# Chunk 0 of a fused attention and expert kernel: up-projection 3 by seven products, banks of its own for each unit, and two turns by transposing transfers

## The chip, the cores and the metric

The kernel runs on one core of a Trainium2 chip. The metric is the device time of one execution in microseconds (us); the profile's span is a little shorter than that time. The engines are named as in the profile: PE (TensorE, the matmul engine), PEld (its weight load), DVE (VectorE), ACT (ScalarE), POOL (GpSimd) and SP (SyncE, which here only issues transfers). PSUM is the memory that PE writes its results to; it has eight banks, and one bank holds 128 x 512 numbers of 4 bytes. SBUF is the large on-chip memory.

## The reference

Attention over pooled keys and values, and then four experts whose outputs are added with weights:

```python
# q, k, v: 8 batches, 8 heads, 576 tokens, 64 dims
k_p = k.reshape(B, H, 72, 8, D).mean(axis=3)      # 72 pooled keys
v_p = v.reshape(B, H, 72, 8, D).mean(axis=3)
attn = softmax(scale * q @ k_p.T)                 # written out in the original
x = (attn @ v_p).transpose(0, 2, 1, 3).reshape(4608, 512)
p = domain_probs / (domain_probs.sum(-1, keepdims=True) + 1e-09)
for e in range(4):
    h = np.maximum(x @ w1[e], 0.0)                # 512 -> 1024
    out += p[:, e:e + 1] * (h @ w2[e])            # 1024 -> 512
```

## The kernel before

**Chunks.** The 4608 tokens are worked in nine chunks of 512. Chunk b, for b from 0 to 7, is the first 512 tokens of batch b; the ninth collects the remaining 64 tokens of each batch. While PE works on the experts of one chunk, the attention of the next batch is woven in between. Everything is bf16 with sums in fp32. For each chunk and expert there is an up-projection (x @ w1[e], the relu, kept in a buffer H) and a down-projection (H @ w2[e], added into acc with the expert's probability).

**Seven products.** Most projections are done by a Strassen-like scheme: a 2 x 2 block product by seven block products instead of eight, at the price of sums of blocks. For an up-projection these are `first_weight_sums(e)` (sums of blocks of w1[e], on DVE), `x_sum(c, n)` (four sums of blocks of x, on DVE) and `up_product(c, e, unit, step)` for step 0 to 6 and unit 0 and 1, each of 4 matmuls of 256 columns (line 681). A unit works in two PSUM banks. What ends a step is: step 0, ACT copies bank 0 into bank 1 (line 694); steps 2 and 3, ACT copies bank 0 to SBUF (`partial`, line 696; in chunk 0 the copies lie in `partial_first`, which is the room of w2[3]); steps 1 and 5, ACT takes the relu (lines 698 and 702); steps 4 and 6, DVE adds a copy and takes the relu (`relu_sum`, line 661). A down-projection is `down(c, e, step)`, seven steps of 8 matmuls (line 749), with `weight_sums(e)` and `hidden_sums(c, e, part)` on DVE. The plain forms are `up` (one fc is 4 matmuls of 512 columns into one bank, line 603) and `down_plain(c, e, r)` (8 matmuls of 512 columns into `chains[r % 2]`, line 775, then an `add` on DVE, line 825).

**Order.** The order of the instructions on each engine is the order in which the program writes them; nothing is moved by a scheduler. Each engine works its list from top to bottom. Waits come from the use of tiles: a matmul that writes a bank waits until the last reader of that bank is done, a reader until the data are there.

**PSUM.** The eight banks are `att` (two), `att_first` (two, in the beginning), `units[1]` (two) and `chains` (two, named o_ps). `units[0]` is allocated only behind chunk 0, in the room that `att_first` leaves. So in chunk 0, `up_product` with unit 0 uses the two banks of `att_first`.

**Chunk 0.** `attention_first()` makes batch 0's attention and the first up-projection, and `first_chunk()` the rest, an order written out by hand: the up-projections 1 (plain), 2 (seven products on both units, the local helper `both(step)`) and 3 (plain, on `units[1]`), the down-projections 0 (seven products), 1 and 2 (plain), and in between the attention of batch 1: `fold_keys(1)`, `queries(1, pair)` (four transposes of a pair of heads on PE and a copy, line 356 and 360), `keys(1)` (line 299), `scores(1, pair)` (line 374, exps on ACT), `context(1, r)` for the four parts r of 128 tokens (line 448, then two DVE instructions of `divide` write `x_tok`, lines 409 and 410), and `turn(1, r)`: four transposes of x_tok on PE (line 466), and a copy by ACT (line 468) into `xT`, the input of chunk 1's up-projections. `two_banks(b)` gives scores and contexts of batches 0 and 1 `att` and `att_first` in turn, and later batches `att`.

From batch 2 on, a turn is a transposing transfer issued by SP, which writes xT straight from x_tok (line 462):

```python
if b >= BUSY:
    nc.sync.dma_start_transpose(out=dst, in_=x_tok)
    return
```

**Loads.** Weights, keys, values and queries are loaded by POOL's queue in the order of the program. `load_w2(3)` follows `both(6)`, since w2[3]'s room is `partial_first` until then; behind it in the queue are `load_wide`, `load_q(2)` and others of batch 2, which wait for `fold_rest`.

**Behind chunk 0** a loop over slots g runs: at slot 0 `up_product(1, 0, 0, 0)` and then `down_plain(0, 2, 3)`; at each later slot two up_products and one `down` step, with pieces of the attention (`later`) and weight sums (`sums`) put at slots of their own. Before the loop, `open_bank` runs one matmul into a bank of the new units[0].

Of the kernel before, what the change touches and what calls it, by code (L numbers as in the profile page):

```python
# [17 lines left out]
def kernel(  # L18
# [231 lines left out]
    def turn_of(what, n):  # L250
        turns[what] += 1
        return turns[what] % n
# [5 lines left out]
        return units[1][turn_of("work", 2)][:]  # L258

    def two_banks(b):  # L260
        return att_first[turn_of("att", 2)] if b < 2 else att

    def one_bank(b):
        return spare_bank() if b == 0 else two_banks(b)[:, 0]
# [25 lines left out]
    def keys(b, hs):  # L290
        state[("kpT", b)] = kpTs[b % 3]
        if b >= BUSY:
            nc.sync.dma_start_transpose(
                out=state[("kpT", b)][:, 0:H], in_=kp_all[:].rearrange("j h a d -> j (h a d)")
            )
            return
        kpt_ps = one_bank(b).bitcast(BF16)[:, 0:H * SP].rearrange("p (h j) -> p h j", j=SP)
        for h in range(hs.start, hs.stop):
            nc.tensor.transpose(kpt_ps[:, h, :], kp_all[0:SP, h], ident[:SP, :SP])
        copy = nc.scalar.copy if b else nc.vector.tensor_copy  # L300
        copy(out=state[("kpT", b)][:, hs, 0:SP], in_=kpt_ps[:, hs])
# [26 lines left out]
        for _ in range(n):  # L328
            nc.tensor.matmul(w_ps[:, 0:cols], lhsT=zeros[:, 0:P], rhs=zeros[:, 0:cols])

    def open_bank(ps):

        nc.tensor.matmul(ps, lhsT=ident[:], rhs=w1_bf[:, 0, 0, 0:NT], skip_group_check=True)

    def values_folds(b):
        raw = raw_v if b >= BUSY else raws[("vraw", b)]
        return (folds(raw) if b < BUSY else []) + [lambda: nc.vector.tensor_add(
# [4 lines left out]
    def queries(b, pair=0):  # L342
        q_sb = raws[("q", b)]
        if pair == 0:
            state[("qT", b)] = apool.tile([P, H, 2, P], BF16, name="qT")
        if b >= BUSY:
            nc.sync.dma_start_transpose(
                out=state[("qT", b)][:].rearrange("p h a t -> p (h a) t"),
                in_=q_sb[:].rearrange("p h r d -> p (h r d)"),
            )  # L350
            return
        bank = one_bank(b) if b else att_first[pair % 2][:, 0] if pair >= 2 else chains[(pair + 1) % 2][:]
        qt_ps = bank.bitcast(BF16)[:, 0:4 * P].rearrange("p (h a t) -> p h a t", h=2, a=2)
        for hh in range(2):
            for rr in range(2):
                nc.tensor.transpose(
                    qt_ps[:, hh, rr, :], q_sb[:, 2 * pair + hh, 2 * rr:2 * rr + 2, :], ident[:]
                )
        copy = nc.scalar.copy if pair in ((1, 3), (1, 2))[b] else nc.vector.tensor_copy
        copy(out=state[("qT", b)][:, 2 * pair:2 * pair + 2], in_=qt_ps)  # L360

    def key_columns(b, h, lo):

# [24 lines left out]
            func=ACT.Exp, scale=EXP_SCALE,  # L388
        )

    def scores_of_two(b, pair):


        scores(b, pair, 0)
        banks = [unit[1][:] for unit in units]
        score_products(b, pair + 1, banks)
        for r2 in range(2):
            nc.scalar.activation(
                out=state[("expT", b)][:, 2 * pair + 2:2 * pair + 4, :, r2].rearrange("j h a t -> j (h a) t"),
                in_=banks[r2][0:SP].rearrange("j (h t) -> j h t", t=P),  # L400
                func=ACT.Exp, scale=EXP_SCALE,
            )
# [53 lines left out]
    def turn(b, r):  # L456
        if ("xT", b) not in state:
            state[("xT", b)] = xpool.tile([P, KC, NT], BF16, name="xT")
        x_tok = state.pop(("x", b, r))[:].rearrange("p a h d -> p (a h d)")
        dst = state[("xT", b)][:, :, r * P:(r + 1) * P]  # L460
        if b >= BUSY:
            nc.sync.dma_start_transpose(out=dst, in_=x_tok)
            return
        xt_ps = (units[1][0][:] if b else att_first[1][:, 0] if r == 3 else chains[0][:]).bitcast(BF16)[:, 0:KC * P].rearrange("p (k t) -> p k t", t=P)
        for kc in range(KC):
            nc.tensor.transpose(xt_ps[:, kc, :], x_tok[:, kc * P:(kc + 1) * P], ident[:])
        copy = nc.vector.tensor_copy if b == 0 and r == 3 else nc.scalar.copy
        copy(out=dst, in_=xt_ps)
# [194 lines left out]
    def up_product(c, e, unit, step):  # L663
        b11, b21, t3, b22 = weight_parts(e)
        a11, _, a12, a22 = x_parts(c)
        t, s, s3 = wu_bf[:, e], state[("xs", c)], third_sum(c)
        banks = units[unit] or [att_first[1][:, i] for i in range(2)]
        bank, grows, lhs, rhs = [
            (0, False, b11, a11),
            (1, True, b21, a12),  # L670
            (0, True, t[:, 1], s[:, 1]),
            (0, True, t3, s3),
            (1, False, t[:, 0], s[:, 0]),
            (0, True, t[:, 2], a22),
            (1, True, b22, s[:, 2]),
        ][step]
        ps = banks[bank][:]
        for n in range(2):
            for kc in range(HK):
                f = (2 * unit + n) * P  # L680
                nc.tensor.matmul(  # L681
                    ps[:, n * HN:(n + 1) * HN], lhsT=lhs[:, kc, f:f + P], rhs=rhs[:, kc, :],
                    start=(not grows and n == 0 and kc == 0), stop=(kc == HK - 1),
                    skip_group_check=True,
                )
        part = (partial if c else partial_first)[:, unit]
        H_sb = hidden[(c, e)]

        def quarter(f, tok):
            return H_sb[:, f, tok, 2 * unit:2 * unit + 2, :].rearrange("p i n -> p (i n)")  # L690

        if step == 0:

            nc.scalar.copy(out=banks[1][:], in_=ps)  # L694
        elif step == 2 or step == 3:
            nc.scalar.copy(out=part[:, step - 2], in_=ps)  # L696
        elif step == 1:
# [154 lines left out]
    def first_chunk():  # L852
# [5 lines left out]

        sums = {e: first_weight_sums(e) for e in range(E)}

        def both(step):
            for unit in range(2):
                up_product(0, 2, unit, step)

        each(*(lambda n=n: x_sum(0, n) for n in range(4)), *sums[0][0:3])
        norm_probs()
# [2 lines left out]
        hidden_sums(0, 0, 1)  # L869
        up(0, 1, (2, 3))  # L870
        each(*sums[1][0:3])
        up(0, 1, (4,), bank=att_first[1][:, 1])
        each(sums[2][0], sums[2][1], sums[2][3], sums[2][2])
        up(0, 1, (5,), bank=chains[0])
        both(0)
        up(0, 1, (6,), bank=chains[1])
        both(1)
        up(0, 1, (7,), bank=chains[0])
        last_sum = weight_sums(0)
        each(sums[0][3], sums[1][3], *last_sum[0:2])  # L880
        both(2)
        down(0, 0, 0)
        both(3)
        hidden_sums(0, 0, 2)
        down(0, 0, 1)
        both(4)
        hidden_sums(0, 0, 3)
        down(0, 0, 2)
        both(5)
        each(*last_sum[2:])  # L890
        down(0, 0, 3)
        both(6)
        load_w2(3)
        up(0, 3, (0,), bank=units[1][0])
        down(0, 0, 4)
        sums[3][0]()
        fold_keys(1)
        up(0, 3, (1, 2, 3))
        down(0, 0, 5)
        sums[3][1]()  # L900
        down(0, 0, 6)
        up(0, 3, (4,))
        queries(1, 0)
        queries(1, 1)
        sums[3][2]()
        up(0, 3, (5,))
        keys(1, every)
        queries(1, 2)
        up(0, 3, (6,))
        queries(1, 3)  # L910
        up(0, 3, (7,))
        scores(1, 0)
        scores(1, 1)
        each(*weight_sums(1)[0:3])
        down_plain(0, 1, 0)
        fold_first, *fold_rest = values_folds(1)
        fold_first()
        scores(1, 2)
        scores(1, 3)
        each(*fold_rest)  # L920
        load_wide(0, 0)
        load_q(2)
# [20 lines left out]
        each(*weight_sums(3)[0:3])  # L943
        down_plain(0, 2, 2)
        turn(1, 3)
        each(*(lambda n=n: x_sum(1, n) for n in range(4)))

    def pieces_later():


        at, amid = {}, {}

        def put_amid(slot, piece):
            amid[slot] = piece
# [59 lines left out]
    with tc.manual_schedule(  # L1014
# [13 lines left out]
        load_w2(0)  # L1028
        load_w1(3)
        attention_first()  # L1030
        load_whole(1, k, "kraw")
        load_q(1)
        load_w2(1)
        load_whole(1, v, "vraw")
        load_w2(2)
        first_chunk()
        psum_first.__exit__(None, None, None)
        psum_last = ctx.enter_context(
            tc.tile_pool(name="psum_last", bufs=1, space=bass.MemoryType.PSUM))
        units[0] = [psum_last.tile([P, NT], F32, name=f"unit0{i}") for i in range(2)]  # L1040
        open_bank(units[0][1][:])

        N = len(order)
        later, amid = pieces_later()
        below_of = [(0, 3)] + order
        sums = {}
        for at, pieces in (((3,), weight_sums(3)[3:]), ((8,), weight_sums(1)[3:]), ((10, 15, 22, 14), weight_sums(2)),
                           ((15,), first_weight_sums(3)[3:])):  # L1050
            for slot, piece in zip(at, pieces, strict=True):
                sums.setdefault(slot, []).append(piece)
        POOLED = (4,)
# [55 lines left out]
```

The softmax here doesn't subtract the row's maximum and nothing guards it: scores larger than these inputs give would overflow.

## Time and profile before

The time before is 491.87 us, the median of 3 runs (491.71 to 492.28). The profiled execution spans 489.4 us.

| | busy us | share of the span |
|---|---|---|
| PE | 481.7 | 98% |
| PEld | 410.3 | 84% |
| DVE | 376.7 | 77% |
| ACT | 304.3 | 62% |
| POOL | 116.4 | 24% |

PE and PEld overlap: the next weights are loaded while a matmul runs. The busy time of matmuls overlaps too, as they are pipelined: the profile gives a matmul of 256 columns 273 ns, though in a dense stretch the next one begins sooner. So the cost of a group of matmuls is read from start to start. A line of the timeline gives the start, the duration, the engine, the source line, the operation, output and inputs, the shape and the count; "idle before" in brackets is what the engine waited for. In the stage that is changed, PE goes through up-projection 3 from 40.5 us, the scores of batch 1 about 51.3 and 53.7, the contexts and turns between 57.7 and 66.6, and chunk 1 from 66.8.

### The profile page before, as it was taken

How to read it: one execution, taken by the hardware profiler on the slowest of the kernel's cores; microseconds unless marked ns; L12 is line 12 of the kernel's file. 1: busy time of each engine (PE TensorE's matmuls, PEld its weight loads, DVE VectorE, ACT ScalarE, POOL GpSimd, SP SyncE). 2: the span in 40 equal slices, each digit the busy share in tenths (PEclk: the TensorE clock that was granted, in tenths of full speed). 3: DMA queues.
4: the chain of work that ended last, by engine and by line, in shares of the span. 5: the costliest groups of instructions: out<-in, count | busy, mean ns of one | idle time of the engine just before them, and what ended most of it. 6: DMA issues, size and time to landing. Idle time of an engine off the chain costs nothing.

```text
span 489.4 us, 11544 instructions
## 1 busy us (share of the span) xinstructions
PE 481.7 (98%) x4694; PEld 410.3 (84%) x4701; DVE 376.7 (77%) x758; ACT 304.3 (62%) x580; POOL 116.4 (24%) x115
## 2 busy tenths in 40 slices
PE   8999999999999999999999999999999999999996
PEld 4867568898888888888889888888888888888885
DVE  5778799799768976798679866897678766876674
ACT  4776546855685567657665567556755566556650
POOL 8320323242423055015321452111011101010100
PEclk9999999999999999999999999999999999999999
DMA  9999998995887579544954298311111010004003
GB/s 196 212 209 205 197 173 127 110 89 62 96 116 60 88 74 139 45 79 54 163 50 90 26 158 74 68 23 65 35 23 23 23 66 2 13 21 87 1 1 87
DMA packets 101828, 41.97 MB, mean 86 GB/s; under 512 B 73856, under 2 KB 100224, under 8 KB 101776
## 3 DMA queue, kind: packets, MB, share of 16 engines
q0 software_dynamic: 56944, 22.42, 41.5%
q1 hardware_dynamic: 43728, 17.77, 16.5%
q10 hardware_dynamic: 1104, 1.05, 0.6%
q8 instruction: 37, 0.61, 0.5%
q14 instruction: 15, 0.12, 0.1%
HBM read 45.69 MB, written 9.44 MB: 113 GB/s over the span
## 4 chain that ended last, share of the span: by engine, by line
PE 96%; POOL 1%; DMA 1%; issue 0%; DVE 0%; POOLq 0%
PE o_ps L749 41%; PE unit L681 41%; PE o_ps L775 3%; PE unit L603 2%; PE att L448 1%; PE unit L808 1%; DMA wt_bf<-in_v_dram 1%; PE att L374 1%; PE o_ps L603 1%; POOL wt_bf L141 1%; PE unit L618 1%; PE att_first L681 1%; PE unit L374 0%; PE o_ps L618 0%; PE att L502 0%
## 5 line engine op out<-in xcount | busy, mean ns | idle before, releaser
L825 DVE SCALAR_TENSOR_TENSOR acc<-o_ps,p_all,acc 128x256 f32<-128x256 f32 (+1 forms) x285 | 127.0, 485 | 52.5 <-PE o_ps L749 37.9
L749 PEld LDWEIGHTS <-H 128*128 128x128 bf16 x1320 | 129.1, 98 | 15.2
L681 PEld LDWEIGHTS <-w_bf 128*128 128x128 bf16 x1056 | 102.2, 98 | 12.7 <-issue 0.2
L661 DVE CUSTOM_DVE_ANT_0 H<-unit,partial 128x512 bf16<-128x512 f32 x128 | 87.2, 684 | 26.1 <-ACT partial L696 12.6
L749 PE MATMUL o_ps<-w_bf,H 128*128 128x256 bf16 x792 | 102.6, 273 | 0.0
L681 PE MATMUL unit<-xT,w_bf 128*128 128x256 bf16 x680 | 97.5, 273 | 0.0
L696 ACT COPY partial<-unit 128x512 f32<-128x512 f32 x128 | 72.3, 592 | 30.0 <-PE unit L681 30.0
L763 POOL TENSOR_TENSOR acc<-acc,addend 128x512 f32<-128x512 f32 x24 | 30.4, 1265 | 253.7 <-ACT addend L761 203.3
L681 PEld LDWEIGHTS <-wu_bf 128*128 128x128 bf16 x792 | 75.3, 98 | 11.4 <-issue 2.5
L681 PE MATMUL unit<-xs,wu_bf 128*128 128x256 bf16 x512 | 77.0, 273 | 0.0
L749 PE MATMUL o_ps<-wt_bf,H 128*128 128x256 bf16 x528 | 68.4, 273 | 0.0
L698 ACT ACTIVATE H<-unit 128x512 bf16<-128x512 f32 x64 | 38.8, 606 | 31.5 <-PE unit L681 31.5
L749 PEld LDWEIGHTS <-S 128*128 128x128 bf16 x528 | 51.7, 98 | 6.2
L702 ACT ACTIVATE H<-unit 128x512 bf16<-128x512 f32 x64 | 38.5, 602 | 25.8 <-PE unit L681 25.6
L694 ACT COPY unit<-unit 128x512 f32<-128x512 f32 x65 | 37.8, 582 | 22.0 <-PE unit L681 17.3
L681 PE MATMUL unit<-xs,w_bf 128*128 128x256 bf16 x256 | 38.4, 273 | 0.0
L823 ACT ACTIVATE acc<-o_ps,p_all 128x256 f32<-128x256 f32 x72 | 30.6, 485 | 10.3 <-PE o_ps L749 8.5
L151 POOL DMA_DIRECT2D kraw<-in_k_dram x20 | 26.4, 1319 | 41.8 <-DMA kraw<-in_k_dram 41.8
L681 PE MATMUL unit<-xT,wu_bf 128*128 128x256 bf16 x228 | 34.2, 272 | 0.0
L749 PE MATMUL o_ps<-w_bf,S 128*128 128x256 bf16 x264 | 34.2, 273 | 0.0
L749 PE MATMUL o_ps<-wt_bf,S 128*128 128x256 bf16 x264 | 34.2, 273 | 0.0
L151 POOL DMA_DIRECT2D vraw<-in_v_dram x20 | 28.9, 1443 | 18.2 <-DMA vraw<-in_v_dram 17.7
(170 smaller groups left out, 517.6 us busy)
## 6 DMA issues: line engine op xcount, KB each, us to landing
out_dram<-acc SPq DMA_DIRECT2D x32, 256.0 KB, 4.6
w_bf<-in_moe_w_dram POOLq DMA_DIRECT2D x6, 1024.0 KB, 20.7
q_sb<-in_q_dram POOLq DMA_DIRECT2D x7, 512.0 KB, 10.0
vraw<-in_v_dram POOLq DMA_DIRECT2D x22, 144.0 KB, 6.6
kraw<-in_k_dram POOLq DMA_DIRECT2D x21, 144.0 KB, 6.3
w_bf<-in_moe_w_dram POOLq DMA_DIRECT2D x4, 512.0 KB, 13.5
wt_bf<-in_k_dram POOLq DMA_DIRECT2D x4, 144.0 KB, 5.7
wt_bf<-in_v_dram POOLq DMA_DIRECT2D x4, 144.0 KB, 4.5
```

Source lines behind the costliest of these rows:

```text
L151: nc.gpsimd.dma_start(out=raw[:], in_=rows_of(src, b, 2 * part, 2 * part + 2), accum_op=ALU.add if part else ALU.bypass)
L603: nc.tensor.matmul(out_ps, lhsT=w1_bf[:, e, kc, fc * P:(fc + 1) * P], rhs=xT[:, kc, at], start=(kc == 0), stop=(kc == KC - 1), skip_group_ ...
L661: nc.vector._custom_dve(TENSOR_ADD_SAT, out=dst, in0=ps, in1=part, s0=LARGEST, s1=0.0)
L681: nc.tensor.matmul(ps[:, n * HN:(n + 1) * HN], lhsT=lhs[:, kc, f:f + P], rhs=rhs[:, kc, :], start=(not grows and n == 0 and kc == 0), stop ...
L694: nc.scalar.copy(out=banks[1][:], in_=ps)
L696: nc.scalar.copy(out=part[:, step - 2], in_=ps)
L698: nc.scalar.activation(out=quarter(0, 0), in_=ps, func=ACT.Relu)
L702: nc.scalar.activation(out=quarter(0, 1), in_=ps, func=ACT.Relu)
L749: nc.tensor.matmul(ps[:, j], lhsT=lhs[:, i, j * P:(j + 1) * P], rhs=rhs[:, i, :], start=(not grows and i == 0 and j == 0), stop=(i == HF - 1),
L763: nc.gpsimd.tensor_add(out=dst, in0=dst, in1=addend[:])
L823: nc.scalar.activation(out=dst, in_=o_ps, func=ACT.Copy, scale=prob)
L825: nc.vector.scalar_tensor_tensor(out=dst, in0=o_ps, scalar=prob, in1=dst, op0=ALU.mult, op1=ALU.add,)
```

## The change

There are four parts.

1. Up-projection 3 of chunk 0 is made by seven products on both units, instead of 32 plain matmuls of 512 columns. `both(e, step)` now takes the expert, and goes through units 1, 0 for expert 3. The four sums of w1[3]'s blocks are all made in chunk 0; the last of them stood at slot 15. `load_w2(3)` follows `both(3, 6)`, which is the last use of `partial_first`.
2. `units[0]` is allocated before chunk 0's second half, and `att_first` is given back there. Both units have banks of their own in chunk 0, and `open_bank` goes. Batch 1's attention then has `att` alone: the queries go four heads at a time through one bank (`queries_of_two`), the keys through `chains[1]`, the scores two pairs at a time through `att` and bank 0 of both units (`scores_of_two`, which later batches have already), and the contexts all through `att`.
3. `turn(1, 0)` and `turn(1, 1)` become transposing transfers; `turn(1, 2)` and `turn(1, 3)` stay on PE.
4. `x_sum(1, 3)` moves from the end of `first_chunk` behind the work of slot 0.

Its purpose is to have fewer and shorter matmuls on PE between the second half of chunk 0 and chunk 1.

```diff
     def two_banks(b):
-        return att_first[turn_of("att", 2)] if b < 2 else att
+        return att if b else att_first[turn_of("att", 2)]
...
-        kpt_ps = one_bank(b).bitcast(BF16)[:, 0:H * SP].rearrange("p (h j) -> p h j", j=SP)
+        kpt_ps = (chains[1][:] if b else spare_bank()).bitcast(BF16)[:, 0:H * SP].rearrange("p (h j) -> p h j", j=SP)
...
-    def open_bank(ps):
-
-        nc.tensor.matmul(ps, lhsT=ident[:], rhs=w1_bf[:, 0, 0, 0:NT], skip_group_check=True)
...
+    def queries_of_two(pair, bank, copy):
...
+        for hh in range(4):
+            for rr in range(2):
+                nc.tensor.transpose(
+                    qt_ps[:, hh, rr, :], q_sb[:, 2 * pair + hh, 2 * rr:2 * rr + 2, :], ident[:]
+                )
+        copy(out=state[("qT", 1)][:, 2 * pair:2 * pair + 4], in_=qt_ps)
...
-    def scores_of_two(b, pair):
-        scores(b, pair, 0)
-        banks = [unit[1][:] for unit in units]
+    def scores_of_two(b, pair, bank=1):
+        scores(b, pair, 0 if b > 1 else None)
+        banks = [unit[bank][:] for unit in units]
...
-        if b >= BUSY:
+        if b >= BUSY or (b == 1 and r < 2):
             nc.sync.dma_start_transpose(out=dst, in_=x_tok)
             return
...
-        banks = units[unit] or [att_first[1][:, i] for i in range(2)]
+        banks = units[unit]
...
-        def both(step):
-            for unit in range(2):
-                up_product(0, 2, unit, step)
+        def both(e, step):
+            for unit in (1, 0) if e == 3 else (0, 1):
+                up_product(0, e, unit, step)
...
-        both(6)
-        load_w2(3)
-        up(0, 3, (0,), bank=units[1][0])
-        down(0, 0, 4)
-        sums[3][0]()
-        fold_keys(1)
-        up(0, 3, (1, 2, 3))
-        down(0, 0, 5)
-        sums[3][1]()
-        down(0, 0, 6)
-        up(0, 3, (4,))
-        queries(1, 0)
-        queries(1, 1)
-        sums[3][2]()
-        up(0, 3, (5,))
-        keys(1, every)
-        queries(1, 2)
-        up(0, 3, (6,))
-        queries(1, 3)
-        up(0, 3, (7,))
-        scores(1, 0)
-        scores(1, 1)
+        both(2, 6)
+        each(*sums[3][0:2])
+        both(3, 0)
+        down(0, 0, 4)
+        both(3, 1)
+        each(sums[3][3], sums[3][2])
+        fold_keys(1)
+        down(0, 0, 5)
+        both(3, 2)
+        down(0, 0, 6)
+        both(3, 3)
+        queries_of_two(0, att[:, 0], nc.scalar.copy)
+        both(3, 4)
+        both(3, 5)
+        keys(1, every)
+        queries_of_two(2, chains[0][:], nc.vector.tensor_copy)
+        both(3, 6)
+        load_w2(3)
+        scores_of_two(1, 0, 0)
         each(*weight_sums(1)[0:3])
         down_plain(0, 1, 0)
         fold_first, *fold_rest = values_folds(1)
         fold_first()
-        scores(1, 2)
-        scores(1, 3)
+        scores_of_two(1, 2, 0)
         each(*fold_rest)
...
-        each(*(lambda n=n: x_sum(1, n) for n in range(4)))
+        each(*(lambda n=n: x_sum(1, n) for n in range(3)))
...
-        at, amid = {}, {}
+        at, amid = {0: [lambda: x_sum(1, 3)]}, {}
...
         attention_first()
+        psum_first.__exit__(None, None, None)
+        psum_last = ctx.enter_context(
+            tc.tile_pool(name="psum_last", bufs=1, space=bass.MemoryType.PSUM))
+        units[0] = [psum_last.tile([P, NT], F32, name=f"unit0{i}") for i in range(2)]
...
         first_chunk()
-        psum_first.__exit__(None, None, None)
-        psum_last = ctx.enter_context(
-            tc.tile_pool(name="psum_last", bufs=1, space=bass.MemoryType.PSUM))
-        units[0] = [psum_last.tile([P, NT], F32, name=f"unit0{i}") for i in range(2)]
-        open_bank(units[0][1][:])
...
-        for at, pieces in (((3,), weight_sums(3)[3:]), ((8,), weight_sums(1)[3:]), ((10, 15, 22, 14), weight_sums(2)),
-                           ((15,), first_weight_sums(3)[3:])):
+        for at, pieces in (((3,), weight_sums(3)[3:]), ((8,), weight_sums(1)[3:]), ((10, 15, 22, 14), weight_sums(2))):
```

More of the change, by code (lines that the diff above doesn't have):

```diff
@@ L351, in queries @@
             return
-        bank = one_bank(b) if b else att_first[pair % 2][:, 0] if pair >= 2 else chains[(pair + 1) % 2][:]
+        bank = att_first[pair % 2][:, 0] if pair >= 2 else chains[(pair + 1) % 2][:]
         qt_ps = bank.bitcast(BF16)[:, 0:4 * P].rearrange("p (h a t) -> p h a t", h=2, a=2)
@@ L358, in queries @@
                 )
-        copy = nc.scalar.copy if pair in ((1, 3), (1, 2))[b] else nc.vector.tensor_copy
+        copy = nc.scalar.copy if pair % 2 else nc.vector.tensor_copy
         copy(out=state[("qT", b)][:, 2 * pair:2 * pair + 2], in_=qt_ps)
+    def queries_of_two(pair, bank, copy):
+        q_sb = raws[("q", 1)]
+        if pair == 0:
+            state[("qT", 1)] = apool.tile([P, H, 2, P], BF16, name="qT")
+        qt_ps = bank.bitcast(BF16)[:, 0:8 * P].rearrange("p (h a t) -> p h a t", h=4, a=2)
+        for hh in range(4):
[4 more added lines that the diff above has]
+        copy(out=state[("qT", 1)][:, 2 * pair:2 * pair + 4], in_=qt_ps)
     def key_columns(b, h, lo):
@@ L871, in first_chunk @@
         each(*sums[1][0:3])
-        up(0, 1, (4,), bank=att_first[1][:, 1])
+        up(0, 1, (4,), bank=units[0][1][:])
         each(sums[2][0], sums[2][1], sums[2][3], sums[2][2])
         up(0, 1, (5,), bank=chains[0])
-        both(0)
+        both(2, 0)
         up(0, 1, (6,), bank=chains[1])
-        both(1)
+        both(2, 1)
         up(0, 1, (7,), bank=chains[0])
@@ L880, in first_chunk @@
         each(sums[0][3], sums[1][3], *last_sum[0:2])
-        both(2)
+        both(2, 2)
         down(0, 0, 0)
-        both(3)
+        both(2, 3)
         hidden_sums(0, 0, 2)
         down(0, 0, 1)
-        both(4)
+        both(2, 4)
         hidden_sums(0, 0, 3)
         down(0, 0, 2)
-        both(5)
+        both(2, 5)
         each(*last_sum[2:])
         down(0, 0, 3)
-        both(6)
-        load_w2(3)
-        up(0, 3, (0,), bank=units[1][0])
-        down(0, 0, 4)
-        sums[3][0]()
-        fold_keys(1)
-        up(0, 3, (1, 2, 3))
-        down(0, 0, 5)
-        sums[3][1]()
-        down(0, 0, 6)
-        up(0, 3, (4,))
-        queries(1, 0)
-        queries(1, 1)
-        sums[3][2]()
-        up(0, 3, (5,))
-        keys(1, every)
-        queries(1, 2)
-        up(0, 3, (6,))
-        queries(1, 3)
-        up(0, 3, (7,))
-        scores(1, 0)
-        scores(1, 1)
+        both(2, 6)
[15 more added lines that the diff above has]
+        both(3, 6)
+        load_w2(3)
+        scores_of_two(1, 0, 0)
         each(*weight_sums(1)[0:3])
```

## The prediction

> **What bounds the kernel now.** I read the page first, for the busy shares and the chain that ended last.
>
> ```profile
> PE 481.7 (98%) x4694; PEld 410.3 (84%) x4701; DVE 376.7 (77%) x758; ACT 304.3 (62%) x580; POOL 116.4 (24%) x115
> ...
> DMA  9999998995887579544954298311111010004003
> ...
> PE 96%; POOL 1%; DMA 1%; issue 0%; DVE 0%; POOLq 0%
> ```
>
> PE is 98% busy and 96% of the chain, so a change is worth the PE time it removes, less the PE waits it brings. The second row says that the DMA engines are full in the first seven slices, some 85 us, and the change puts two transfers there. Next, busy time by stretches:
>
> ```profile
> 40.50:66.80 26.30, 25.98 (x200) 14.66 (x203) 21.87 (x39) 12.76 (x22) 6.46 (x8) 1.00 1.30 199
> ...
> 80.00:470.00 390.00, 390.00 (x3813) 344.15 (x3812) 302.49 (x609) 251.89 (x483) 87.62 (x75) 1.00 0.49 66
> ```
>
> The columns are the stretch, its length, then PE, PEld, DVE, ACT and POOL busy, clock, DMA share, GB/s. The changed stretch is 40.5 to 66.8. From 80 us on PE has no gap at all: whatever the change makes of the moment when chunk 1's first up_product starts (66.79) is carried unchanged to the end. So I compute that moment. PE's timeline has the pieces:
>
> ```profile
> 40.54 1.03 PE L603 MATMUL unit<-xT,w_bf 128*128 128x512 bf16 x3
> ...
> 42.28 2.75 PE L603 MATMUL unit<-xT,w_bf 128*128 128x512 bf16 x12
> 44.87 1.04 PE L749 MATMUL o_ps<-w_bf,H 128*128 128x256 bf16 x8
> 45.74 1.04 PE L749 MATMUL o_ps<-wt_bf,H 128*128 128x256 bf16 x8
> ...
> 66.35 0.39 PE L466 MATMUL unit<-ident,x_tok 128*128 128x128 bf16 x4
> 66.58 0.38 PE L333 MATMUL unit<-w_bf,ident 128*128 128x512 bf16 x1
> 66.79 0.60 PE L681 MATMUL unit<-xT,w_bf 128*128 128x256 bf16 x4
> ```
>
> Durations overlap, so I price by start to start: twelve of 512 columns in 2.59 us are 216 ns each, eight of 256 in 0.87 us are 109 ns each, one turn (four transposes) is 0.23, open_bank 0.21.
>
> Last, what a transposing transfer takes. Below are stretches around some issues of the existing turns, and the landing of the one at 194.65 and of the one at 162.30:
>
> ```profile
> 61.00:64.00 3.00, 2.95 (x25) 1.64 (x24) 2.94 (x6) 0.59 (x1) 1.76 (x3) 1.00 1.35 195
> 64.00:67.00 3.00, 3.00 (x29) 1.81 (x28) 2.91 (x6) 0.81 (x2) 0.00 (x0) 1.00 1.52 193
> ...
> 194.60:197.60 3.00, 3.00 (x30) 2.70 (x28) 2.64 (x6) 1.36 (x4) 1.18 (x1) 1.00 1.43 88
> ```
>
> ```profile
> xT<-x_tok SPq DMA_TRANSPOSE x1, 5.6
> ...
> xT<-x_tok SPq DMA_TRANSPOSE x1, 2.4
> ```
>
> The median of the 24 is 2.5 us. Those issued while loads ran are slower: 101.34 took 6.9, 143.48 6.3, 194.65 5.6, 298.09 6.0, and 156.56 and 246.84 3.8 and 3.9. Where the new ones fall (59 to 68 us) the share is 1.35 to 1.52, as high as the worst of these.
>
> **What the Trainium skill says.** "DMA: Bandwidth & Descriptors", Queues, rings and completion order: each DMA engine takes turns between the queue rows it has work for, packet by packet. The trace agrees: from 195.8 to 196.3 the loads' queue ran 149 packets and the transposes' 109. The same page, Why a DMA increments its semaphore by 16 and not by 1: every engine posts its own last increment after its data, so the slowest of 16 engines sets the landing; the 5.6 to 6.9 us beside loads fit. "TensorE: Matmul & The Clock Gate", Back-to-back issue gap, gives N/2.4 + 2.5 ns, 109 and 216 ns here: the trace has just that (its other figure, 131 ns for 512 columns in a stream, the trace doesn't bear out).
>
> **The change part by part.**
> PE work. Up-projection 3 was 8 x 4 = 32 matmuls of 512 columns: 6.93 us. As seven products on two units it is 56 of 256: 6.11. Two turns less: 0.45. open_bank gone: 0.21. Sum: 0.82 + 0.45 + 0.21 = 1.48 us less. queries_of_two, keys and scores_of_two do the same transposes and products as before in other banks: nothing on PE.
> Units' own banks before 40.5 us: PE was busy 18.45 of 18.50 us from 22 to 40.5, so nothing to gain.
> Waits inside expert 3. up_product step 1 accumulates onto the copy that ACT makes of step 0, and that copy must wait until DVE's relu_sum of expert 2's step 6 has left the bank (41.01 + 0.68 = 41.69). Two copies at 0.58, the second 0.5 later, end at 42.3 and 42.8; PE comes at 42.28 and 42.7: 0.2 us of waiting, with down(0,0,5) queued behind. The later steps alternate with downs or transposes and find ACT and DVE done.
> More on DVE: four relu_sums of 0.6 (ACT did relus before) and one more weight sum, moved from slot 15. The four queries copies become one of 1024 columns on each of ACT and DVE. By my count DVE ends its last relu_sum at 51.8 (PE ends both(3,6) at 50.8), then three sums of weights 1 (2.1 before: 50.99 to 53.13), an add (0.67), folds and vp (2.3: 54.49 to 56.80) and the add of down_plain(0,1,1) (0.67): 57.5. PE has passed context(1,0) at 57.1 and wants that bank for down_plain(0,1,3): 0.45 us waiting, with context(1,1) behind it.
> att alone for the four contexts: x_tok of one must be out before the next. PE puts 1.73 us of down_plain and 0.26 of context between; add, inv, x_tok on DVE take 0.67 + 0.23 + 0.69 = 1.6. It just fits: nothing.
> Arrival at up_product(1,0,0,0): from 40.54 the old work sums to 25.87 (6.93 + three downs 2.62 + 7 plain 12.12 + contexts 1.04 + turns 0.88 + queries 0.88 + scores 0.92 + keys 0.26 + 0.21), that is 0.38 of gaps in 26.25. The new is 24.4 + 0.2 + 0.45 + 0.15 of small gaps: 65.7 instead of 66.8. Without more, 1.1 us won.
> load_w2(3) must now wait for the last use of partial_first, which lies in it: issued at 52 instead of 42.23. But the loads in this queue land in turn: weights 2 of w2 at 57.8, this one at 63.6 before. Issued at 52 it still stands behind weights 2, and DVE reads it at 65: nothing.
> The two transfers. up_product(1,0,0,0) reads tokens 0 to 255, just turns 0 and 1; PE, in order, stands there, with down_plain(0,2,3) and all of chunk 1 behind it. x_tok(1,1) is out at 61.1 (61.50 before; it gains little as DVE is late). It has 4.6 us until PE arrives. Bounds from the trace: 2.4 (quiet) to 6.9 (loads). I take 6.6, near the upper end: loads fill the engines to beyond 69 us, and turn(1,0), issued at 59.0, stands ahead in the same queue. Landing 67.7, PE starts at 67.75: 2.0 us of waiting against 1.1 won. Net +1.0: 492.9.
> Two ACT copies of turns go (1.2 us), two exps come (0.6 each), x_sum(1,3) goes behind the add of slot 0: ACT is 12.76 of 26.3 busy, and both hide behind PE's wait.
>
> **The rivals.**
> Transfers get through, 490.7: they land within 4.6 us, as at 156.56 and 246.84 (3.8, 3.9). For it: in the trace the transposes' packets are small (256 B), and loads were accumulating in the slow cases, plain here. Against: fuller engines, two in one queue. Then only 1.1 to 1.2 us is won.
> Middle, 491.9: the second takes 5 to 6.2, as at 194.65 and 298.09, landing 66.1 to 67.3. The wait just eats the gain.
> load_w2(3) becomes the wait, 495: if its 21.4 us runs from issue, it lands at 73 and down(0,3,0) (69.83 before) waits some 3 us. Against: the landings in turn.
>
> **How the numbers follow.** Forecast case 47% (41 slower, 6 within 0.2%, as +0.2% is 492.85), middle 22% (18 within, 2 each side), transfers get through 26% (25 faster, 1 within), w2 5% (slower). Faster 0.27, same 0.25, slower 0.48. The range, from 490.6 (all fast) to 494.0 (the second transfer at 7.7), leaves out the w2 case and some tails.
>
> **What would show it.** Right: a PE gap ahead of L691 at 66 to 68 us released by the transfer xT<-x_tok, two such issues near 59 and 61 with 5.5 to 7.5 us to landing, a PE wait near 57 released by a DVE add. Wrong: landings below 4.6 and PE going straight on near 65.7; or DVE waiting for w2.

## The result and the profile after

The changed kernel takes 497.60 us (median of 6 executions, 495.79 to 498.87) against 491.98 for the kernel before (6 executions, 491.71 to 492.31) on the same chip. The ratio is 1.0111, 95% interval 1.0089 to 1.0132: slower by some 5.6 us. Forecast was 492.9, with a range from 490.6 to 494.0. The profiled execution of the changed kernel took 498.32 us, with a span of 496.4.

The page of the changed kernel, the lines that answer to those shown of before, with the granted clock of PE over the 40 slices as well:

```profile
PE 483.7 (97%) x4716; PEld 412.8 (83%) x4716; DVE 378.9 (76%) x761; ACT 303.8 (61%) x581; POOL 116.4 (23%) x115
...
PE   8999969999999999999999999999999999999995
...
PEclk9999979999999999999999999999999999999999
DMA  9999996979496739743983398220211010004003
...
PE 91%; DMA 3%; DVE 2%; POOL 1%; ACT 1%; issue 0%; POOLq 0%; DVEq 0%; ACTq 0%
```

PE is busy for 2 us more than before (483.7 against 481.7), although it has less to do. In the sixth slice (62 to 74 us) it is busy only six to seven tenths of the time, and in the same slice its clock is down. PE's share of the chain fell from 96% to 91%, and DMA's rose to 3%. The chain of waits of the changed kernel between 55 and 80 us has the piece that is new (start, length, what):

```profile
59.52 0.75 DVE acc L835
...
60.42 0.69 DVE x_tok L420
61.11 0.03 DVE S L245
61.14 9.11 DMA xT<-x_tok
70.25 0.04 issue
70.29 1.03 PE unit L691 x4
71.32 3.41 PE o_ps L785 x8
```

and PE's timeline of the changed kernel shows what PE does meanwhile (start, busy time, then the operation, and in brackets the idle time before it and what ended it):

```profile
65.51 0.39 PE L476 MATMUL unit<-ident,x_tok 128*128 128x128 bf16 x4
70.29 1.03 PE L691 MATMUL unit<-xT,w_bf 128*128 128x256 bf16 x4 [4.40 <-DMA xT<-x_tok]
71.12 3.62 PE L785 MATMUL o_ps<-w_bf,partial 128*128 128x512 bf16 x8
74.53 1.68 PE L691 MATMUL unit<-xT,w_bf 128*128 128x256 bf16 x8
76.05 1.04 PE L759 MATMUL o_ps<-w_bf,H 128*128 128x256 bf16 x8
```

Two things are to be seen. PE ends its last turn at 65.9 and stands until 70.29 for the second transfer, issued at 61.14, which took 9.11 us. Then the eight matmuls of down_plain take 3.41 us instead of 1.73. The busy time by stretches says why; the columns are the stretch, its length, busy time of PE, PEld, DVE, ACT and POOL, granted clock, DMA share, GB/s:

```profile
66.00:69.00 3.00, 0.00 (x0) 0.00 (x0) 2.32 (x4) 0.52 (x1) 0.00 (x0) 1.00 1.45 177
69.00:70.00 1.00, 0.00 (x0) 0.00 (x0) 0.00 (x0) 0.00 (x0) 0.00 (x0) 0.50 2.12 163
70.00:73.00 3.00, 2.71 (x9) 1.31 (x10) 0.76 (x2) 0.57 (x1) 0.00 (x0) 0.50 2.06 154
73.00:75.00 2.00, 2.00 (x8) 0.78 (x6) 0.23 (x1) 0.00 (x0) 0.00 (x0) 0.50 2.11 123
75.00:76.00 1.00, 1.00 (x7) 0.72 (x6) 1.00 (x3) 0.31 (x1) 0.62 (x1) 0.58 0.55 78
76.00:79.00 3.00, 3.00 (x30) 2.69 (x29) 1.81 (x4) 2.39 (x5) 0.79 (x1) 1.00 0.76 131
```

While PE stood, its clock was cut to half, from 69.0 to 75.8 us, so that its first 5.5 us of work in chunk 1 went at half speed. For the sum, this is down(0,3,0) in the kernel before:

```profile
69.83 1.04 PE L749 MATMUL o_ps<-w_bf,H 128*128 128x256 bf16 x8
```

Chunk 1 starts at 70.29 instead of 66.79, which is 3.5, and down(0,3,0), which follows 3.04 us after that start before, now follows 5.76 after it, which is 2.7 more. Together that is 6.2 of the 7.0 us by which the two profiled spans differ (496.4 and 489.4). Of the rest, PE loses 0.2 us between 100 and 120 us, and nothing more up to its last down-projection of this kind at 484; what remains lies in the last 12 us.

The six executions fit this. In the two shortest (495.79 and 496.48) the granted clock of the whole execution was 0.996, in the four others (497.56 to 498.87) it was 0.992. A halved stretch of 3.41 us costs half its length, 1.7 us or 0.35% of the whole (an estimate), so the two had one such stretch, and the others two, like the profiled one.

### The profile page after: what moved, and what is told of

Its sections match the earlier page's. It is cut to its first block, busy times and chain, and to the rows that moved or that the text cites. A ratio compares the mean times of both kernels' runs of the same rounds, so it can differ in the third digit from the quotient of the medians.

```text
span 496.4 us, 11589 instructions
## 1 busy us (share of the span) xinstructions
PE 483.7 (97%) x4716; PEld 412.8 (83%) x4716; DVE 378.9 (76%) x761; ACT 303.8 (61%) x581; POOL 116.4 (23%) x115
## 4 chain that ended last, share of the span: by engine, by line
PE 91%; DMA 3%; DVE 2%; POOL 1%; ACT 1%; issue 0%; POOLq 0%; DVEq 0%; ACTq 0%
PE unit L691 41%; PE o_ps L759 39%; PE o_ps L785 2%; DMA xT<-x_tok 2%; PE att L458 1%; PE unit L818 1%; DMA wt_bf<-in_v_dram 1%; DVE acc L835 1%; PE o_ps L613 1%; POOL wt_bf L141 1%; PE att L383 1%; PE unit L613 1%; PE unit L628 1%; PE unit L383 1%; DVE x_tok L420 1%
## 5 line engine op out<-in xcount | busy, mean ns | idle before, releaser
L691 PEld LDWEIGHTS <-w_bf 128*128 128x128 bf16 x1088 | 105.7, 98 | 18.3 <-DMA xT<-x_tok 4.6
L691 PE MATMUL unit<-xT,w_bf 128*128 128x256 bf16 x704 | 101.5, 275 | 4.4 <-DMA xT<-x_tok 4.4
L691 PEld LDWEIGHTS <-wu_bf 128*128 128x128 bf16 x816 | 77.6, 98 | 11.6 <-issue 2.5
L708 ACT ACTIVATE H<-unit 128x512 bf16<-128x512 f32 x66 | 39.9, 605 | 33.9 <-PE unit L691 33.9
L704 ACT COPY unit<-unit 128x512 f32<-128x512 f32 x68 | 39.4, 581 | 27.7 <-PE unit L691 22.2
L712 ACT ACTIVATE H<-unit 128x512 bf16<-128x512 f32 x66 | 39.6, 602 | 26.1 <-PE unit L691 25.8
L691 PE MATMUL unit<-xT,wu_bf 128*128 128x256 bf16 x240 | 35.7, 272 | 0.0
```

The lines of the kernel that those rows point to most:

```text
L691: nc.tensor.matmul(ps[:, n * HN:(n + 1) * HN], lhsT=lhs[:, kc, f:f + P], rhs=rhs[:, kc, :], start=(not grows and n == 0 and kc == 0), stop ...
```

## The experiments

The theory that these started from: the second transfer is late because loads hold it up, the clock adds about as much again, and the seven products by themselves save what the prediction said. The rivals: the seven products or the changed banks lose time of their own, or transfers of this kind simply take 9 us. Each kernel is compared with the kernel before, run on the same chip; the medians of before there were 491.5 to 491.8.

**All four turns on PE.** The changed kernel without its third part.

```diff
-        if b >= BUSY or (b == 1 and r < 2):
+        if b >= BUSY:
```

> The changed kernel with all four turns of batch 1 on PE again (part 3 undone), the other parts kept. Theory A (the two transfers are the whole loss): PE goes straight into chunk 1 at about 66.2 us (65.7 of the changed kernel plus two turns of 0.23), 0.6 us earlier than in the kernel before, the clock stays whole, 491.4 us. Theory B (the banks, the seven products or DVE's longer queue cost as well): more than 492.5 us.

Measured: 492.52 against 491.66, ratio 1.0025 (1.0013 to 1.0038). Neither expectation is met whole: the number is just that of Theory B, but the time isn't lost where B looks for it. The loss of 5.6 us is gone, but not a microsecond is won. PE does come to chunk 1 early, and then stands at slot 6. The lines of PE at that place, first of the kernel before, then of this one:

```profile
79.53 0.41 PE L485 MATMUL att<-qTr,kpT 64*128 64x64 bf16 x16
```

```profile
79.95 0.41 PE L495 MATMUL att<-qTr,kpT 64*128 64x64 bf16 x16 [1.53 <-DMA qTr<-q_rem]
```

This is rem_scores, which needs the transposing transfer qTr. In the kernel before, qTr came just in time, without a PE gap; a PE that is earlier has to wait for it. So "carried unchanged to the end" was wrong: the lead ends at the next transfer. In 7 of the 20 executions it cost more: they took 494.1 to 495.4 us at a granted clock of 0.995 or 0.996, the 13 others 491.6 to 492.9 at 0.997 or more. By the estimate above that is one halved stretch, though only an execution without it was profiled.

**The two transfers alone.** The kernel before with the third part only (the condition of the diff above, put into before).

> The kernel before with only turns 0 and 1 of batch 1 made transfers (part 3 alone); the load of w2[3] is then issued at 42 us. Theory A1 (the transfers' packets run once the packets of the w2[3] load are through, about 61 us here): second landing near 68, PE waits 1.5 to 2 us, no halved clock, 493.3 us. Theory A2 (a transfer here takes 9 us from its issue whatever is loaded): second landing at 70.6, PE waits over 4 us, the clock is halved, 498 us.

Measured: 497.25, ratio 1.0110 (1.0086 to 1.0134), the whole loss of the change. The transfers landed 10.2 and 9.9 us after issue; PE's line:

```profile
70.97 1.03 PE L681 MATMUL unit<-xT,w_bf 128*128 128x256 bf16 x4 [4.99 <-DMA xT<-x_tok]
```

So the third part alone brings the whole loss, without the seven products and the banks.

**The gap filled.** The changed kernel with 20 idle matmuls of 512 columns ahead of chunk 1, 4.3 us of PE work that nothing reads.

```diff
+        idle(20, units[1][1][:])
         N = len(order)
```

> The changed kernel with 20 idle matmuls of 512 columns (20 x 0.216 = 4.3 us) in the gap ahead of chunk 1, so that PE waits only some tenths of a us. Theory A (the loss is the wait of some 3.5 us net and then the halved clock of some 2.8 us, which the gap sets off): the clock stays whole, 2.8 us less than the changed kernel, 495 us. Theory B (the clock falls for another cause, or the wait alone is the loss): 497.6 us as before and the half clock still there.

Measured: 495.57 against 491.66, ratio 1.0087 (1.0055 to 1.0119). The gap ahead of chunk 1 is 1.1 us, and the same stretches as above show a whole clock:

```profile
69.00:70.00 1.00, 0.57 (x3) 0.08 (x1) 0.51 (x2) 0.00 (x0) 0.00 (x0) 1.00 2.29 155
70.00:73.00 3.00, 2.31 (x14) 1.30 (x15) 0.76 (x2) 0.57 (x1) 0.00 (x0) 1.00 2.02 155
```

PE's lines at chunk 1's start and at down(0,3,0):

```profile
70.69 0.61 PE L691 MATMUL unit<-xT,w_bf 128*128 128x256 bf16 x4 [1.12 <-DMA xT<-x_tok]
...
73.74 1.04 PE L759 MATMUL o_ps<-w_bf,H 128*128 128x256 bf16 x8
```

Chunk 1 starts no earlier (70.69), but down(0,3,0) follows after 3.05 us, as before, and not after 5.76. That is the halved clock's 2.7 us, shown in the trace by taking it away. The times bear it out less well: this kernel is 3.9 us above before and the changed one 5.6, but the two intervals overlap. Its profiled execution, 497.92, was the longest of four, and loses 1.6 us again in two later waits, 0.38 at 83.9 and 1.19 at 126.0.

**Only the first turn by transfer.** The changed kernel with turn(1, 1) back on PE.

```diff
-        if b >= BUSY or (b == 1 and r < 2):
+        if b >= BUSY or (b == 1 and r < 1):
```

> The changed kernel with turn 0 alone as a transfer, turn 1 on PE. Theory Q (two transfers in one queue share the blame): the one lands at about 66, just when PE arrives (65.95), 491.3 us. Theory L (each transfer by itself takes over 8 us there, as the first one's 8.4): it lands at 67.5, PE waits 1.5 us, 492.7 us. In both the gap is too short to halve the clock.

Measured: 496.4, ratio 1.0105 (1.0063 to 1.0147). PE stands 1.72 us for that transfer ahead of chunk 1, and 1.66 us for qTr at slot 6. One transfer is late as well, so the queueing of the second behind the first isn't the main cause.

**What holds the transfers up: the cut of one load.** In the changed kernel no packet of the transposing queue ran before 63.0, just when the 1024-byte packets of load_w2(3) ended. So this load was cut into four.

```diff
-        n = 1 if e else 2
+        n = 4 if e == 3 else 1 if e else 2
```

> The changed kernel with load_w2(3) cut into four transfers of a quarter each; nothing else moves. In the changed kernel no packet of the transposing queue ran before 63.0 us, just when the last 1024-byte packet of that load was through. Theory P (a DMA engine works off the whole run of one load before it takes the other queue): with four shorter runs the first transposing packets come at 60 to 61.5, the second transfer lands near 68 instead of 70.3, PE waits some 2 us and the clock stays whole: about 493. Theory S (the engines are simply full up to 63, and the cut of the load is nothing to them): the first packets again near 63, landings after 8 to 10 us, 496 to 498.

Measured: 497.81, ratio 1.0119; first packet at 63.05, landings after 9.1 and 9.6 us, a gap of 4.88. Cutting the load changes nothing.

**The loads behind held back.** GpSimd issues the eight loads only when both transfers have landed.

```diff
-        load_wide(0, 0)
-        load_q(2)
...
         turn(1, 3)
+        nc.gpsimd.tensor_copy(out=gate[:], in_=state[("xT", 1)][:, :, 0:NT // 2:P])
+        load_wide(0, 0)
+        load_q(2)
...
```

> The changed kernel with the eight loads that follow load_w2(3) (load_wide, load_q(2), load_q_rem) held back until both transposing transfers have landed, by a small GpSimd copy that reads their result. Only the landing of the two transfers is judged; the whole time must suffer, since queries, keys and values of batch 2 come later. Theory W (load_w2(3) alone holds the transfers up, and what follows it is harmless): first transposing packet near 63 as before, but then alone: landings near 65 and 67. Theory L (the loads behind are the cause): the first packet comes at once after the issue at 59, landings within 4 us of issue. Theory N (neither; two transfers of this kind in one queue take 9 us): landings again at 67.5 and 70.3.

Measured: the first packet came 1.4 us after issue, where it was 3.9 in the changed kernel, and the transfers landed 6.4 and 4.8 us after issue, at 64.8 and 65.2. PE went on at 65.21, within 0.1 us of the end of its last turn. (The time was 503.0: with batch 2's loads late, PE stood at 73.7 for 2.2 us and at 82.0 for 5.8.) The DMA view from 59 to 63 us, by queue (q0 carries the loads, q1 the transposes; packets, MB, share), of the changed kernel and then of this one:

```profile
q0 software_dynamic: 1029, 0.77, 123.0%
```

```profile
q0 software_dynamic: 499, 0.50, 75.8%
q1 hardware_dynamic: 351, 0.09, 55.0%
...
xT<-x_tok SPq DMA_TRANSPOSE x2, 5.6
```

The transposing queue has no line at all in the changed kernel, and 351 packets here. In both kernels load_w2(3)'s packets went on to 63 or a little beyond; only here nothing stood behind it. So the loads behind are what holds the transfers up (Theory L), though the landings stay above the 4 us that it gave.

**GpSimd's issuing.** In four runs the first packet came 0.2 to 0.3 us after GpSimd's last load issue, so its issuing itself was suspected. Three kernels: load_q(2) and load_q_rem issued at 52 us; tiny loads in place of the held ones; and load_q early with the load_wide held back by a copy behind x_tok(1,2).

```diff
         load_w2(3)
+        load_q(2)
+        load_q_rem(0)
+        load_q_rem(1)
```

> The changed kernel with load_q(2) and the two load_q_rem issued right behind load_w2(3), at 52 to 55 us, so that GpSimd issues only the four load_wide after 57.2 and is through at 60.5 instead of 62.8. The bytes that stand in the load queue are the same. Theory D (a transposing transfer gets no packet while GpSimd is in a row of load issues; in four runs the first packet came 0.2 to 0.3 us after the last issue ended): first packet near 60.8, landings 2 us sooner, 65.5 and 68.3, PE waits 2.5 us or less, 493.5 to 495.5. Theory B (the bytes queued ahead hold it up): first packet near 63 as before, landings 67.5 and 70.3, 497 to 498.

```diff
+        for n in range(16):
+            nc.gpsimd.dma_start(out=tiny[:, n], in_=moe_domain_probs[n * P:(n + 1) * P, 0:2])
```

> The earlier kernel that holds the eight loads back until the transfers have landed (landings 64.9 and 65.4 there), with sixteen tiny loads of 8 bytes a partition into a tile that nothing reads, issued by GpSimd one after the other from 52.5 to some 65 us. They carry 16 KB in all. Only the landings are judged. Theory D (GpSimd's issuing holds the transposing transfers up): no transposing packet until the row of issues ends near 65, landings at 67 or later. Theory B (the bytes queued do it): first packet 1.4 us after issue as in that kernel, landings near 65.

```diff
         context(1, 2)
+        nc.gpsimd.tensor_copy(out=gate[:], in_=state[("x", 1, 2)][:, 0, 0, 0:2])
+        load_wide(0, 0)
...
```

> The changed kernel with load_q(2) and load_q_rem issued right behind load_w2(3) and the load_wide held back to 63.8 us by a small GpSimd copy that reads x_tok(1,2); qTr goes ahead of qT, and queries(2) to slot 1. No issue of GpSimd falls between 55 and 63.8. Theory D: both transfers start within 1.5 us of their issue and land before 66, PE passes slot 0 without a gap, qTr is early; if the wide loads come in time the kernel keeps the whole saving of PE, 489.5 to 490.2. Theory B: landings at 67 or later, 494 or more. In between: the transfers land in time but keys or values of batch 2 come late, 491 to 494, with the gap at slots 4 to 9.

Measured: 497.85 (1.0127), first packet at 62.61, landings after 9.1 and 9.9; 507.7 in a single execution, landings after 7.5 and 5.6; 496.93 (1.0098), first packet at 62.32, landings after 8.1 and 8.2. The third decides: GpSimd issued no load from 54.8 to 63.1, and still no transposing packet ran before 62.32. Its DMA view from 59 to 62 us has the loads' queue alone:

```profile
q0 software_dynamic: 721, 0.59, 125.9%
```

Issuing is not the cause. The tiny loads don't bear on it as meant, since GpSimd stood in its row of issues from 56.5 to 59.6 and from 60.1 to 64.9, waiting for a load to land; they show only that loads of few bytes behind do little harm: with six of them queued the first packet came 1.5 us after issue, and PE waited 0.92 us.

**Any load, or this one?** load_w2(3) held back until the transfers have landed, the seven others at their place.

```diff
-        load_w2(3)
...
+        nc.gpsimd.tensor_copy(out=gate[:], in_=state[("xT", 1)][:, :, 0:NT // 2:P])
+        load_w2(3)
         turn(1, 2)
```

> The changed kernel with load_w2(3) held back, by a small GpSimd copy, until both transposing transfers have landed, and the seven loads after it issued as before from 57 us. So when the transfers are issued, the queue holds load_wide, load_q(2) and load_q_rem alone. Only the landings are judged; sums of weights 3 come late and the whole time must suffer. Theory V (what holds a transposing transfer up is any load that stands queued behind the one in work; its engines go on to that load first): first packet again 3 us or more after issue, landings 7 us or more after issue. Theory X (it is load_w2(3), with its long row of 1024-byte packets, together with what is behind it): first packet about 1.4 us after issue as with nothing behind, landings within 6.5 us.

Measured: landings after 10.4 and 9.7 us, first packet 4.9 us after issue. The DMA view from 59 to 63 us again has loads only:

```profile
q0 software_dynamic: 734, 0.51, 103.2%
...
xT<-x_tok SPq DMA_TRANSPOSE x2, 10.1
```

So load_w2(3) isn't needed for it. Taken together, the pairs of transfers landed 4.8 to 6.4 us after issue with one load under way and nothing behind, 8.1 and 8.2 with only load_q(2) and load_q_rem behind it until 63 us, and 8.4 to 10.4 with seven or eight loads behind. So, at this place, loads queued behind the one under way delay the transfers.

It isn't their number. In the changed kernel the transfer of qT, issued at 72.42 with five loads not landed, got its first packet after 1.24 us; but only 0.24 MB of these loads were left to move (issued by GpSimd, their packets not started). At 59.07, when the first turn was issued, it was 1.64 MB. In the traces up to 80 us the eleven transposing transfers issued with 0.97 to 2.1 MB left, with no transposing packet under way, got their first packet after 3.9 to 4.9 us, those with 0.26 MB or less after 1.2 to 1.3, and those in between after 1.3 to 3.0. This is an order that the traces show; no experiment varied the amount alone.

**Room for qTr.** Two ways to give the early PE its qTr, both on the kernel with all turns on PE. One has rem_scores one slot later:

```diff
-            ... rem=(0, 6, 8, 14),
+            ... rem=(0, 7, 8, 14),
```

> The changed kernel with all four turns of batch 1 on PE (as in the earlier experiment of that kind, 492.5) and rem_scores of batch 2's plan moved from slot 6 to slot 7, because PE stood 1.5 us at slot 6 for the transposing transfer qTr. Theory Q (that transfer takes back what the seven products save): the gap near 80 us goes, PE keeps its lead of 0.7 to 1 us, 490.7 to 491.1, 0.6 to 1 below the kernel before. Theory R (the wait only moves, since rem_context in slot 8 now follows closely on the exponentials): a gap of about the same size one or two slots later, 492 or more.

The other has load_q_rem ahead of the wide loads (taken from its place behind them) and queries(2) in slot 1, so that qTr is issued ahead of qT:

```diff
+        load_q_rem(0)
+        load_q_rem(1)
         load_wide(0, 0)
...
-            queries=0, keys=4,
+            queries=1, keys=4,
```

> All four turns of batch 1 on PE again, rem_scores left in slot 6, but load_q_rem(0) and (1) issued ahead of the wide loads and the transposing transfer qTr issued ahead of qT (queries moved to slot 1). Theory Q (qTr is late only because it stands behind qT, which waits for load_q(2)): qTr lands before 76, no gap at slot 6, 490.7 to 491.1. Against it: the gap stays, since the transfers take 6 to 9 us wherever they stand, and qT becomes late for the scores of slot 9: 492 or more.

Measured: 490.61 against 491.79, ratio 0.9975 (0.9965 to 0.9985), and 490.29, ratio 0.9970 (0.9949 to 0.9991). Both beat the kernel before. PE has no gap in chunk 1's first slots; in the second kernel rem_scores comes without one, at

```profile
78.25 0.41 PE L495 MATMUL att<-qTr,kpT 64*128 64x64 bf16 x16
```

The control is the kernel before with the second pair of moves.

> Control: the kernel before with load_q_rem(0) and (1) ahead of the wide loads and qTr ahead of qT, the same two moves that made the version with all turns on PE faster. Before had no PE gap at slot 6. If the gain there came from the seven products and the moves only let it through, before stays at its time within 0.1%. If the moves are faster by themselves, it gains 0.5 us or more.

Measured: 491.32 against 491.51, ratio 0.9997 (0.9989 to 1.0006). The moves alone are worth nothing; they let through what the seven products save. The later rem_scores of the other kernel has no such control.

**A transfer with a later reader.** The faster kernel with one turn by transfer, that of tokens 256 to 383, issued first. The contexts go in the order 2, 0, 1, 3.

```diff
-        if b >= BUSY:
+        if b >= BUSY or (b == 1 and r == 2):
```

> The fastest version so far (all turns on PE, load_q_rem and qTr ahead, 490.3) with one turn of batch 1 by a transposing transfer, but that of the tokens 256 to 383, which only x_sum(1,0) reads: contexts in the order 2, 0, 1, 3, and turn(1,2) issued first, near 59. By the theory that the transfer lands some 8 to 9 us after issue whatever is done, it lands at 67 to 68, x_sum follows at 68, and step 2 of the first product finds its sums near 69: it just fits, and PE keeps one turn, 0.23 us: 490.0 to 490.3. If it lands at 68.5 or later, PE waits at step 2 by as much: 490.5 to 492.

Measured: 491.87, ratio 1.0006 (0.9996 to 1.0017); it gives the gain back, and the expectation is missed. The transfer landed at 67.5 as expected, but PE stood 0.68 us up to 69.17, for DVE: x_sum waits for the transfer in DVE's queue, and the add behind it comes late. It stood another 0.54 us up to 71.62, for ACT. A third gap, 2.16 us up to 93.0 behind ACT, stands in the one profile of it too, an execution of 496.1 and so not typical; how much of this a typical execution has stays open.

## Why the prediction was wrong

The side was right, the size was not: 497.6 where the range ended at 494.0.

- *Arrival at up_product(1,0,0,0): 65.7.* Right: 65.7. From the start of expert 3 to that point PE took 26.25 us before and 25.05 now, 1.2 less against 1.1 forecast. That the arrival agrees to the tenth is in part chance, as expert 3 started 0.15 us later than before. DVE's add held down_plain(0,1,3) to 57.59, some 0.2 us of waiting where 0.45 was put; the other small waits weren't measured one by one. Two slips in the working change nothing: its old work adds up to 25.86 and not 25.87, and the DMA row is full in six slices, as the seventh reads 8.
- *load_w2(3), nothing.* Right: issued at 52.39, landed at 65.2, no wait of DVE on it. The rival built on it, 495, was the nearest to the time, for a wrong reason.
- *x_tok(1,1) out at 61.1.* Right: 61.11, issue at 61.14.
- *"I take 6.6, near the upper end".* This step failed. The transfer took 9.11, beyond the upper bound of 6.9, and its wait was 4.4 instead of 2.0. The bound came from transfers in other places, by the share of busy DMA alone; what stood in the load queue wasn't asked for. At the six transfers that the prediction lists as slow, 0.15 to 0.3 MB of loads were left to move; at 61.14 it was 1.68 MB. Holding the queued loads back gave 6.4 and 4.8, which is the forecast's own range; with loads queued, the pairs of seven kernels took 8.1 to 10.4.
- *The sum.* It had no term for the clock. The wait of 4.4 us brought the half clock on, and that cost 2.7 us in the trace, which were gone when the gap was filled. The Trainium skill, in "TensorE: Matmul & The Clock Gate", What's actually happening, has the array's clock fall to half after an idle window of about 3.4 us. The traces agree on the length, halved stretches of 3.41 or 6.83 us after gaps of up to 6.2 us, and on the half, 427 ns a matmul of 512 columns where it was 216. But they show it after shorter gaps too: of 2.15 us, in the kernel that held the loads back, and 2.16, in the last of the experiments. The measurement decides: 2.0 us of idle time within one window were enough (the last section has the working), and the longest gap that left the clock whole, 1.72 us, was split between two windows. The forecast wait of 2.0 was next to that edge, and the longer waits that the range took in were past it; both wanted a term for it.
- *"Carried unchanged to the end".* Wrong, though hidden here: with the turns on PE, qTr took the lead back at slot 6 (1.53 us). PE without a gap from 80 us on wasn't free of what other engines do; a transfer that lands just in time leaves no record of a wait.

The saving by the seven products is real. Of the 1.2 to 1.5 us that the two faster kernels win, 0.76 is seen from the start of expert 3 to chunk 1 (25.49 against 26.25); the rest lies ahead of that, where the records shift by up to a microsecond between executions, and isn't settled.

The same skill, in "DMA: Bandwidth & Descriptors", Queues, rings and completion order, on which the prediction rested, has an engine take turns between the queues that it has work for. From 63 us on the trace shows that, with 1068 transposing packets beside 1324 of the loads up to 69. For the 4 us before, it shows none of the transposes' at all. Whether the transposing queue had nothing ready then, or had and wasn't served, no record tells.

## What to carry to other kernels

Before a transfer takes work off a busy engine, price it in its own place: not by how full the DMA engines are, but by how much of the loads stands queued when it is issued, and then ask whether its reader can wait that long. If PE could stand idle for some 2 us, put the cost of the halved clock into the sum. A kernel without a gap may still have transfers that land just in time, so when PE gets earlier, look for the next one and move its issue forward as well.

## What the runs showed of the hardware

- With loads queued behind the load under way, 1.1 to 2.1 MB in all, a transposing transfer of 128 x 512 issued at 58 to 59 us got its first packet only 3.9 to 4.9 us after issue (nine kernels), against 1.4 with 0.64 MB of one load left and nothing behind. Cutting the load, or keeping GpSimd from issuing, changed little.
- The clock changed only on a grid of 3.41 us. In all sixteen traces each stretch of whole or half clock, from the first whole one to the end of the work, was a whole number of 3.413 us long; in the changed kernel 64.85 us whole (19), 6.83 half (2), 419.84 whole (123). Laid over these windows, PE's idle time tells what followed, without an exception: whole clock after windows with at most 1.89 us idle, half clock after those with 2.01 us or more; and a half clock ended after windows with at most 0.60 us idle, and went on after those with 0.84 or more.
- So the length of a gap alone doesn't tell: gaps of 2.15, 3.48 and 4.99 us were followed by one stretch of 3.41 us, those of 4.40, 4.88, 5.16 and 5.18 by one of 6.83. After the gap of 3.48 the half clock began 1.1 us after PE was at work again, at the end of the window that had held 2.37 us of idle time.
- Of sixteen tiny loads in a row, behind two loads of weights that had not landed, GpSimd issued six, and then waited 3.1 us, and after one more 4.8 us, for those loads of weights before it issued the rest.
